# Two transformer layers on one core: VectorE takes the third bank of some score units, with new ranks for the instruction planner

## Chip, cores and metric

The kernel runs on one core of a Trainium2 chip. The metric is device time in microseconds (us): the median of the runs of one program. Engine names in the profile: PE is TensorE's matmuls and PEld its weight loads, DVE is VectorE, ACT is ScalarE, POOL is GpSimd, SP is SyncE (here it issues DMAs).

## What is computed

Two identical layers work on x, a sequence of 2048 rows of 448. Each layer is an attention block (16 heads of 28) and then a mixer block with a gelu MLP (inner size 1792). Inputs and output are bf16.

```python
def _A_ref(x, wqkv, wo):                     # attention
    q, k, v = ...                            # x @ wqkv, 16 heads of 28
    scores = jnp.einsum("bhqd,bhkd->bhqk", q, k) * (Dh ** -0.5)
    p = _softmax(scores, axis=-1)
    o = jnp.einsum("bhqk,bhkd->bhqd", p, v)
    return (heads of o side by side) @ wo
def _B_ref(x, w1, w2, w3, w4):               # mixer and MLP
    h = _gelu(_layernorm(x) @ w1)
    ... # the four quarters of h's columns, shifted by +1, -1, +2, -2 rows
    x1 = x + hs                              # hs = shifted h @ w2
    return x1 + _gelu(_layernorm(x1) @ w3) @ w4
# the whole, twice:
x = x + _A_ref(_layernorm(x), A_wqkv, A_wo)
x = x + _B_ref(_layernorm(x), B_w1, B_w2, B_w3, B_w4)
```

## The kernel before, in words

**Work.** The 2048 rows are 16 tiles of 128. The 16 heads are four groups g of four heads (j = 0 to 3). Queries are taken in chunks of tiles (`CHUNKS`): per layer L three of four tiles, ch 0 to 2, and two of two tiles, ch 3 and 4. `ORDER` cuts each chunk's keys into ranges, so that attention can begin before all keys exist. One range of one chunk for one g is a segment; `segs` lists 32 segments of layer 0 and then 36 of layer 1. A segment's scores come in blocks of 128 keys by 512 columns of one head: 512 queries, or twice 256 with two key tiles in the two-tile chunks. Four blocks, one for each j, make a key block kb. There are 1024 blocks per layer, 2048 in `stream`.

**Score units.** `t_scores` (from L1440) walks the stream. Even units take three blocks in PSUM banks 0, 1, 2, odd units two blocks in banks 3, 4 (`unit_banks`). `score_ops` (L1311) issues their matmuls, the blocks of a unit side by side on different rows of the array. `t_exp` (L1541) exponentiates a whole unit with one ScalarE activation from PSUM into the buffer PT, which holds six units. The scores of unit u wait for the exponential of unit u-2, and the exponential of unit u for PV of unit u-6. `t_pv` (L762 is the line of its matmuls, which come from the helper `mm`) multiplies by V in bank 5. `t_norm` copies the sums out (L1620, L1622) and divides by the softmax's denominator.

**Exponentials on VectorE.** For some blocks VectorE computes the exponential. At each unit, `t_scores` looks 5 or 6 key blocks ahead. If in the planner's account PE spent 15% or more of the last 8 us on filler (`FTH`), the segment has had fewer than `D_RATE[L, ch] * (kb + 1) * 4` such blocks, at most two (`DPK`) of the key block are taken, and a spare bank (b6 or b7), an integer buffer y and an output buffer pd are free, that block is scored with the unit and leaves the stream. Only four-tile chunks take part. `d_first` (L1393) turns the scores into integers in y and releases the bank; `d_chain` (L1431, L1433, L1435, L1438) evaluates a cubic and puts the exponent bits in. Two y buffers exist; more y, f and pd buffers lie in parts of vaug (V with a column of ones) that are unused at the time (`t_extra`): phase 0 up to segment 16, phase 1 after the last PV of layer 0 (event kvfree) up to segment 61. A second branch of `d_chain` on POOL has all its rates at 0.

**The rest of a layer.** After a chunk's attention, `t_outproj` adds the output projection (L1700), `t_mixA` does the first half of the mixer (gelu through tanh with POOL, VectorE and ScalarE, L1787 to L1790), and `t_mixB` the second half for a group of tiles (`BGROUPS`: 0-2, 3-6, 7-10, 11-12, 13-15): `t_mixB1` per tile, then W3 in 14 pieces of 128 features, each with a bank of its own and a VectorE cast (L1933) into h2T, one wide gelu on ScalarE (L1955), and W4 with the residual. In layer 1 a second buffer for it ("h2W") is made of slots of vaug and kT. After the last exponential ("tail") ScalarE takes gelu directly from PSUM (L1929). `t_ln1_l1` normalizes tiles for layer 1 and stores them by DMA.

**What sets the order.** The order of each engine's instructions is written at build time by a planner (`Sched`, a list scheduler with costs in us for every operation). Every piece of work is a generator, spawned with a rank; of candidates that could start at about the same time the lower rank goes first. The ranks of Q, K/V, mixer halves and the rest come from `RANK`, 1.1 to 2.8 in steps of 0.05 over a list of 35 (kind, L, ch); scores have 0, PV 1. The planner also fills PE's idle time with matmuls on the identity (L1996, `keep_pe_busy`). At run time each engine works its list in order, with semaphore waits from the planner's read and write sets.

## Time and profile before

| what | us |
|---|---|
| three runs: median, lowest, highest | 1064.31, 1063.14, 1071.81 |
| span of the profiled execution, first to last instruction | 1061.2 |
| the median less that span | 3.1 |
| ScalarE busy | 1017.8 |
| of it exponentials (L1541, 803 instructions) | 919.4 |
| PE busy, of it filler (L1996) | 990.3, 144.8 |
| VectorE busy, POOL busy | 628.6, 309.1 |
| first exponential starts, last ends | 17.5, 1017.4 |

The profiled execution is one of its own; of it the span is known, and the time around the span is taken as the 3.1 us that separate it from the median. In the profile, "xN" is a count, the figures after a bar are busy us and mean ns of one instruction, and the figures after the second bar are the idle time of the engine just before them and what ended it. Means of one instruction include overlap with the next, so the busy time of a group is less than count times mean.

### The profile page before, as it was taken

Reading aid. Unit: us, or ns where it says so; the run is one execution under the profiler, and the core shown is the slowest. Engines: PE = TensorE matmul, PEld = TensorE weight load, DVE = VectorE, ACT = ScalarE, POOL = GpSimd, SP = SyncE. Lnnn points to the kernel's source line nnn. Section 1 sums busy time; section 2 is a strip of 40 time slices with the busy share of each in tenths; the row PEclk is TensorE's granted clock in tenths of the full one; section 3 lists DMA queues with packets and bytes.
Section 4 is the critical chain, followed back from the end, with each engine's and each line's share of the span. In section 5 each row is a group of like instructions: output and inputs, shape, how many; then the busy total and the mean of one; then the engine's idle time right before and its main releaser. Section 6 shows DMA issues by size and latency. Waiting matters only on the chain.

```text
span 1061.2 us, 34191 instructions
## 1 busy us (share of the span) xinstructions
PE 990.3 (93%) x15418; PEld 405.6 (38%) x15421; DVE 628.6 (59%) x1275; ACT 1017.8 (96%) x921; POOL 309.1 (29%) x510
## 2 busy tenths in 40 slices
PE   6999999989999899999999999999899999999898
PEld 2333433333333444443333333343233334444465
DVE  7777887874574336665455644767686632644433
ACT  6999999999999999999999999999999999999962
POOL 2343112532451022652122301111754300432112
PEclk9999999999999999999999999999999999999999
DMA  4555232230220031220121132423411110221000
GB/s 116 131 131 192 73 65 74 43 66 22 67 60 20 21 96 32 50 38 22 35 86 42 45 91 72 149 69 94 89 25 26 43 38 16 54 54 18 16 15 24
DMA packets 96642, 64.29 MB, mean 61 GB/s; under 512 B 68656, under 2 KB 85376, under 8 KB 96496
## 3 DMA queue, kind: packets, MB, share of 16 engines
q1 hardware_dynamic: 93120, 54.02, 20.2%
q0 software_dynamic: 3376, 8.09, 2.8%
q8 instruction: 121, 1.98, 0.8%
q14 instruction: 25, 0.20, 0.1%
HBM read 28.16 MB, written 16.76 MB: 42 GB/s over the span
## 4 chain that ended last, share of the span: by engine, by line
ACT 75%; PE 16%; DVE 4%; DMA 2%; POOL 1%; issue 1%; SPq 0%; DVEq 0%
ACT PT L1541 68%; PE ps L771 9%; PE ps L1311 4%; ACT h2T L1955 3%; PE ps L762 3%; ACT fb L1789 1%; ACT L1955 1%; ACT L1541 1%; DMA xT<-xnd 1%; DVE st L949 1%; DMA rT<-ub 0%; DMA PT<-in_A_wqkv_dram 0%; DMA xT<-xn 0%; PE ps L1996 0%; ACT vaug L1955 0%
## 5 line engine op out<-in xcount | busy, mean ns | idle before, releaser
L1541 ACT ACTIVATE PT<-ps 128x1536 bf16<-128x1536 f32 (+1 forms) x803 | 919.4, 1342 | 7.1 <-PE ps L1311 6.6
L1311 PE MATMUL ps<-qT,kT 32*128 32x512 bf16 (+1 forms) x2560 | 314.2, 340 | 36.0 <-ACT PT L1541 26.7
L762 PE MATMUL ps<-PT,vaug 128*32 128x512 bf16 (+1 forms) x2518 | 249.2, 340 | 1.0 <-DVE ub L1622 1.0
L1311 PEld LDWEIGHTS ps<-qT,kT 32*128 32x128 bf16 x2560 | 80.5, 91 | 314.4 <-ACT PT L1541 291.8
L771 PE MATMUL ps<-xT,w 128*32 128x512 bf16 (+2 forms) x1952 | 148.3, 357 | 2.9 <-DMA xT<-xn 1.1
L1996 PE MATMUL ps<-ident 128*32 128x256 bf16 x3188 | 144.8, 274 | 2.3 <-POOL ident L851 1.5
L762 PEld LDWEIGHTS ps<-PT,vaug 128*32 128x32 bf16 x2518 | 75.0, 95 | 93.5 <-issue 77.6
L1646 POOL TENSOR_TENSOR otn<-ub,fb 128x512 bf16<-128x512 f32 (+1 forms) x36 | 41.6, 1157 | 236.2 <-DMA fb<-rscr 223.6
L1933 DVE CAST h2T<-ps 128x384 bf16<-128x384 f32 (+2 forms) x98 | 58.3, 595 | 87.7 <-PE ps L771 77.9
L771 PE MATMUL ps<-w,h2T 128*32 128x448 bf16 x1400 | 99.0, 363 | 7.8 <-ACT h2T L1955 7.8
L1996 PEld LDWEIGHTS ps<-ident 128*32 128x32 bf16 x3188 | 89.5, 96 | 28.9 <-issue 12.7
L771 PEld LDWEIGHTS ps<-xT,w 128*32 128x32 bf16 (+1 forms) x1952 | 53.0, 95 | 47.9 <-issue 23.7
L1098 POOL TENSOR_TENSOR sq<-kT 128x512 bf16<-128x512 bf16 (+2 forms) x32 | 30.0, 937 | 116.6 <-DVE kT L1112 114.4
L1787 POOL TENSOR_TENSOR fb<-hT 112x512 f32<-112x512 bf16 (+1 forms) x36 | 37.4, 1042 | 71.7 <-DVE hT L1770 66.3
L771 PEld LDWEIGHTS ps<-w,h2T 128*32 128x32 bf16 x1400 | 37.4, 97 | 42.2 <-issue 15.9
L1098 POOL TENSOR_TENSOR sq<-qT 128x512 bf16<-128x512 bf16 x28 | 29.6, 1060 | 58.7 <-DVE qT L1145 54.2
L1620 DVE COPY ub<-ps 128x512 f32<-128x512 f32 (+1 forms) x40 | 23.3, 583 | 35.0 <-PE ps L762 34.4
L1873 POOL TENSOR_TENSOR x_res<-x_res,x1b 128x448 f32<-128x448 f32 x32 | 38.1, 1193 | 18.6 <-DVE xn L969 18.6
L771 PE MATMUL ps<-xT,wk_pad 128*32 128x512 bf16 (+1 forms) x512 | 42.5, 376 | 0.5 <-DVE kmaxc L1123 0.4
L1700 DVE TENSOR_TENSOR x_res<-x_res,ps 128x448 f32<-128x448 f32 x32 | 19.8, 619 | 38.9 <-PE ps L771 38.6
L771 PE MATMUL ps<-xT,wq_pad 128*32 128x512 bf16 x448 | 41.4, 392 | 0.8 <-DMA xT<-xnd 0.6
L771 PE MATMUL ps<-wo_pad,otn 128*32 128x448 bf16 x512 | 38.9, 361 | 2.5 <-DVE x_res L1700 2.0
(191 smaller groups left out, 1174.0 us busy)
## 6 DMA issues: line engine op xcount, KB each, us to landing
uscr<-ub SPq DMA_DIRECT2D x28, 256.0 KB, 2.0
ub<-uscr SPq DMA_DIRECT2D x28, 256.0 KB
fb<-rscr SPq DMA_DIRECT2D x24, 256.0 KB
xnd<-xn SPq DMA_DIRECT2D x28, 128.0 KB, 2.0
x_res<-in_A_x_dram POOLq DMA_DIRECT2D x16, 224.0 KB, 3.2
xd<-x_res SPq DMA_DIRECT2D x16, 224.0 KB, 2.6
x_res<-xd SPq DMA_DIRECT2D x16, 224.0 KB, 2.8
out_dram<-obf SPq DMA_DIRECT2D x16, 112.0 KB
```

The source lines that it names most:

```text
L762: return lambda e: e.matmul(out=out, lhsT=lhsT, rhs=rhs, start=start, stop=stop, **kw)
L771: r.append(e.matmul(out=out[c:c + w, :], lhsT=lhsT[:, c:c + w], rhs=rhs, start=start, stop=stop, tile_position=(0, c)))
L1098: return op("pool", 0.15 + NW * 0.0018, lambda e: e.tensor_tensor(out=sq[:, si, 0:NW], in0=src, in1=src, op=ALU.mult), reads=rk, writes=[( ...
L1311: yield op("pe", max(0.055, 0.22 / nc_ * NW / 512.0), lambda e, i=i, kc=kc, j=j, g=g, a=a, NW=NW, bank=bank: e.matmul(out=ps[:, bank, i * ...
L1541: yield op("act", 0.06 + n * w * 0.000833, lambda e, bk=bk, s0=s0, n=n, w=w: e.activation(out=PT[:, s0:s0 + n, 0:w], in_=ps[:, bk[0]:bk[0] ...
L1620: yield op("dve", c_ps(NW), lambda e: e.tensor_copy(out=u, in_=ps[:, 5, 0:NW]), reads=[("ps", 5)], writes=[uk])
L1646: yield op("pool", 0.2 + NW * 0.0021, lambda e: e.tensor_tensor(out=otn[:, g, 0:NW], in0=u, in1=rb[:, 0:NW], op=ALU.mult), reads=[uk, fk], ...
L1787: yield op("pool", 0.2 + NW * 0.00165, lambda e: e.tensor_tensor(out=f, in0=z, in1=z, op=ALU.mult), reads=hk, writes=[fk])
L1873: yield op("pool", 1.2, lambda e: e.tensor_tensor(out=X, in0=X, in1=X1, op=ALU.add), reads=[xk, ("x1b", s)], writes=[xk], deps=[nop_])
L1933: ev = op("dve", c_ps(NW), lambda e, hr=hr, vw=vw, b=b: e.tensor_copy(out=hr, in_=vw(ps[:, bi(b), 0:NW])), reads=[("ps", bi(b))], writes=h ...
L1955: yield op("act", c_act(len(fr_) * NW), lambda e, v=v: e.activation(out=v, in_=v, func=ACT.Gelu_apprx_tanh), reads=allk, writes=allk, tab= ...
L1996: return [e.matmul(out=ps[32 * c:32 * c + 32, bi(b), 0:256].rearrange("p (a n) -> p a n", n=128), lhsT=ident[:, 32 * c:32 * c + 32], rhs=i ...
```

## The change

1. **Third bank to VectorE.** In an even unit, before the third block is taken from the stream, the planner's VectorE load over the last 6 us (`DWIN`) is looked up. If it is under 0.7 (`DTH`), a block 5 or 6 key blocks ahead is sought under a second table of rates, `R_RATE`. If y and pd buffers are free, that block's scores go to bank 2, and ScalarE's unit has two blocks. `d_first` doesn't release the bank; it signals dx, and unit u+2 waits for that. For this no filler share and no spare bank are asked for.
2. **Rates of the old way** are new, and the two-tile chunks take part. The POOL branch goes. The chain's rank before it is urgent goes from 1.5 to 2.5.
3. **Own wide buffer.** In layer 0 the W3 result of tiles 11-12 lies in vaug slots 9 to 15 once kvfree has come, instead of in h2T; phase 1 of the extra buffers then opens only when W4 of these tiles is done.
4. **Two-tile W3.** Two 256-column pieces share a bank, and one cast or gelu takes both.
5. **Ranks.** Single values of three decimals in `RANK`. V, LN1 of layer 1, the output projection, `t_mixB1` and W4 (now `t_w4`) get their own ("v", "l", "o", "c", "w"), where they had those of K, K, mixer half A, mixer half B and mixer half B. `Q_LEAD` (how many segments ahead queries are projected) changes too.
6. **Planner.** The costs of 256-column score and PV matmuls change by a few per cent; the bookkeeping of candidates is rewritten without a new rule.

The core of the diff (`RANK` cut to the entries that are spoken of):

```diff
@@ -310,6 +312,14 @@
         self.fills = [x for x in self.fills if x > t]
         return len(self.fills) * 0.12 / win
 
+    def load(self, eng, win):
+        t = self.clock - win
+        busy = 0.0
+        for (e, a, b, _) in reversed(self.log[-150:]):
+            if e == eng and b > t:
+                busy += b - max(a, t)
+        return busy / win
+
     def keep_pe_busy(self, until):
         if self.fill is None:
             return
...
-DPRIO = 1.5
+DPRIO = 2.5
...
-PRATE = {(0, 0): 0, (0, 1): 0, (0, 2): 0, (0, 3): 0, (1, 0): 0, (1, 1): 0, (1, 2): 0}
-XSHUT = (16, 61)
+R_RATE = {(0, 0): 0, (0, 1): 0.01, (0, 2): 0, (0, 3): 0, (0, 4): 0, (1, 0): 0, (1, 1): 0.03, (1, 2): 0.01, (1, 3): 0, (1, 4): 0.04}
+RLO = 5
+RHI = 7
+RPRIO = 1
+DWIN = 6.0
+DTH = 0.7
...
-RANK = {k: round(1.1 + 0.05 * i, 3) for i, k in enumerate([..., ('a', 1, 2), ...])}
+RANK = {..., ('a', 1, 2): 1.166, ..., ('b', 1, 2): 2.769, ('b', 1, 3): 2.461, ..., ('o', 1, 2): 2.439, ('c', 1, 2): 2.409, ('w', 1, 2): 2.844, ('c', 1, 3): 2.317, ('w', 1, 3): 2.98, ...}
-Q_LEAD = {(0, 1): 8, (0, 2): 5, (0, 3): 5, (1, 0): 5, (1, 1): 7, (1, 2): 3, (1, 3): 5}
-D_RATE = {(0, 0): 0.08, (0, 1): 0.045, (0, 2): 0.05, (0, 3): 0, (1, 0): 0.015, (1, 1): 0.1, (1, 2): 0.03}
+Q_LEAD = {(0, 1): 8, (0, 2): 7, (0, 3): 10, (1, 0): 8, (1, 1): 11, (1, 2): 3, (1, 3): 4}
+D_RATE = {(0, 0): 0.1, (0, 1): 0.055, (0, 2): 0.035, (0, 3): 0.03, (0, 4): 0.03, (1, 0): 0.025, (1, 1): 0.095, (1, 2): 0.045, (1, 3): 0.005, (1, 4): 0.045}
...
+SMALL = [11, 12]
...
@@ -1350,7 +1365,7 @@
             return []
 
         def t_extra(ph, base):
-            yield ("wait", ("vinit",) if ph == 0 else ("kvfree",))
+            yield ("wait", ("vinit",) if ph == 0 else ("h2xfree",) if SMALL else ("kvfree",))
             yield ("sig", ("xopen", ph))
             yield ("wait", ("segstart", XSHUT[ph]))
             yield ("sig", ("xshut", ph))
@@ -1388,16 +1403,18 @@
         PDS = ["pd%d" % i for i in range(NPD)]
         YS = ["y0", "y1"]
 
-        def d_first(blk, bank, ys, pd):
+        def d_first(blk, bank, ys, pd, ring=None):
             y, yk = ybuf(ys)
             yield op("dve", c_ps(512), lambda e: e.tensor_scalar(out=y, in0=ps[:, bi(bank), :], scalar1=SCALE * L2E * FS, scalar2=-126.0 * FS, op0=ALU.mult, op1=ALU.max),
                      reads=[("ps", bi(bank))], writes=yk, touch=[bank])
-            yield ("rel", bank)
+            if ring is None:
+                yield ("rel", bank)
+            else:
+                yield ("dead", bank)
+                yield ("sig", ("dx", ring))
             yield ("spawn", d_chain(blk, ys, pd), DPRIO)
 
         at = [0, 0]
-        flying = [0]
-        bypool = set()
 
         def d_chain(blk, ys, pd):
             si, kb, _ = blk
...
@@ -1450,14 +1454,59 @@
             pos = 0
             u = 0
             taken = {}
-            while pos < len(stream):
+
+            def ahead_of(si0, kb0, rates, lo, hi, used):
+                for ahead in range(lo, hi):
+                    si, kb = si0, kb0 + ahead
+                    while si < len(segs) and kb >= len(seg_kb[si]):
+                        kb -= len(seg_kb[si])
+                        si += 1
+                    if si > si0 + DSEG or si >= len(segs):
+                        return None
+                    L, ch, g = segs[si][0:3]
+                    rate = rates.get((L, ch), 0)
+                    if not rate:
+                        return None
+                    js = [j for j in range(4) if (si, kb, j) not in home and j not in used]
+                    if taken.get((si, kb), 0) >= DPK or not js:
+                        continue
+                    if taken.get((si, id(rates), 0), 0) >= rate * (kb + 1) * 4:
+                        continue
+                    if any(("k", L, g, kc_of(L, kt)) not in SC.events for kt in seg_kb[si][kb]):
+                        return None
+                    if si > si0 and (("q", L, CHUNKS[L][ch][0] // 4, g) not in SC.events or (not segs[si][5] and ("qp", si) not in SC.events)):
+                        return None
+                    return (si, kb, js[0])
+                return None
+
+            def take(blk, rates, slot):
+                home[blk] = pbuf(slot)
+                taken[(blk[0], id(rates), 0)] = taken.get((blk[0], id(rates), 0), 0) + 1
+                taken[blk[0:2]] = taken.get(blk[0:2], 0) + 1
+
+            ringed = set()
+            while True:
                 if u == 1:
                     yield ("acq", ["b3"])
                     yield ("acq", ["b4"])
                 if u >= 2:
                     yield ("wait", ("ex", u - 2))
+                if u - 2 in ringed:
+                    yield ("wait", ("dx", u - 2))
                 un = []
-                while pos < len(stream) and len(un) < 3 - u % 2:
+                rb = None
+                lim = 3 - u % 2
+                while pos < len(stream) and len(un) < lim:
+                    if len(un) == 2 and rb is None and SC.load("dve", DWIN) < DTH:
+                        rb = ahead_of(un[-1][0], un[-1][1], R_RATE, RLO, RHI, [b_[2] for b_ in un])
+                        got = None
+                        if rb is not None:
+                            got = yield ("try", [xtra("y") + YS, xtra("pd") + PDS])
+                        if got is not None:
+                            take(rb, R_RATE, got[1])
+                            ringed.add(u)
+                            break
+                        rb = 0
                     blk = stream[pos]
                     pos += 1
                     if blk in home:
...
+                if u in ringed:
+                    blks.append(rb)
+                    banks.append(2)
+                    extra.append((rb, ("b2", got[0], got[1], u)))
+                if SC.idle_share(8.0) >= FTH:
+                    blk = ahead_of(si0, kb0, D_RATE, DLO, DHI, [b_[2] for b_ in blks])
+                    if blk is not None:
                         got = yield ("try", [MISC[0:2], xtra("y") + YS, xtra("pd") + PDS])
+                        if got is not None:
+                            take(blk, D_RATE, got[2])
+                            blks.append(blk)
+                            banks.append(bi(got[0]))
+                            extra.append((blk, got))
                 yield from score_ops(blks, banks)
                 for blk, got in extra:
+                    yield ("spawn", d_first(blk, *got), 1 if len(got) == 3 else RPRIO)
                 yield ("sig", ("st", u))
                 u += 1
             units.append([])
...
@@ -1892,7 +1915,13 @@
                 for xs in slots:
                     yield ("rel", xs)
             wide = False
-            if direct:
+            hname = None
+            small = L == 0 and tiles == SMALL
+            if small:
+                yield ("wait", ("kvfree",))
+                hb = vaug[:, 9:16, :].rearrange("p a b -> p (a b)").rearrange("p (f w) -> p f w", w=NW)
+                hkey = [[("vaug", 9 + k) for k in range(f * NW // 512, (f * NW + NW - 1) // 512 + 1)] for f in range(14)]
+            elif direct:
                 hb, hkey = PT, [[("pt", f)] for f in range(14)]
             else:
                 hname = yield ("acq", ["h2T", "h2W"] if ("xdone", 1) in SC.events else ["h2T"], [("xT", xt)])
...
+            parts = [list(range(f, min(f + fps, 14))) for f in range(0, 14, fps)]
+            if wide:
+                parts = [p for q in parts for p in ([f for f in q if f < 7], [f for f in q if f >= 7]) if p]
+            for fs in parts:
+                m = len(fs)
+                for k, fch in enumerate(fs):
+                    for fc in FCS:
+                        yield op("pe", c_mm(NW), (mm4 if NW > 300 else mm)(ps[:, bi(b), k * NW:(k + 1) * NW], w3[:, fc, 128 * fch:128 * fch + 128], xv(xt)[:, fc, 0:NW], fc == 0, fc == 3),
+                                 reads=[("xT", xt), ("w3",)], writes=[("ps", bi(b))], touch=[b], mode="col4" if NW > 300 else "plain")
+                hk = []
+                for f_ in fs:
+                    hk += [k for k in hkey[f_] if k not in hk]
+                pv = ps[:, bi(b), 0:m * NW].rearrange("p (f w) -> p f w", w=NW)
+                if wide and fs[0] >= 7:
+                    hr = kT[:, 0:n, 128 * (2 + fs[0]):128 * (2 + fs[0] + m)].rearrange("p a (f r) -> p f a r", r=128)
+                    pv = pv.rearrange("p f (a r) -> p f a r", r=128)
+                else:
+                    hr = vaug[:, 9 + fs[0]:9 + fs[0] + m, 0:NW] if wide else hb[:, fs[0]:fs[0] + m, 0:NW]
+                if m == 1:
+                    hr, pv = hr[:, 0], pv[:, 0]
+                    ev = op("dve", c_ps(m * NW), lambda e, hr=hr, pv=pv: e.tensor_scalar(out=hr, in0=pv, scalar1=0.5, scalar2=None, op0=ALU.mult),
+                    ev = op("act", c_act(m * NW), lambda e, hr=hr, pv=pv: e.activation(out=hr, in_=pv, func=ACT.Gelu_apprx_tanh),
+                    late.extend(fs)
+                    ev = op("dve", c_ps(m * NW), lambda e, hr=hr, pv=pv: e.tensor_copy(out=hr, in_=pv),
...
+            yield ("spawn", t_w4(L, tiles, hcol, hkey, late, direct, soft, small, wide, hname), RANK["w", L, ch])
+
+        def t_w4(L, tiles, hcol, hkey, late, direct, soft, small, wide, hname):
-            if not direct:
+            if small:
+                yield ("sig", ("h2xfree",))
+            elif not direct:
...
-                SC.spawn(t_outproj(L, ch), RANK["a", L, ch])
+                SC.spawn(t_outproj(L, ch), RANK["o", L, ch])
```

## The prediction, made before the result was known

> **What bounds the kernel now.** I read the page's first two parts, then the chain of work that ended last, then the costly groups with their shapes kept apart, then busy time by stretches and the tail's timeline.
>
> ```profile
> PE 990.3 (93%) x15418; PEld 405.6 (38%) x15421; DVE 628.6 (59%) x1275; ACT 1017.8 (96%) x921; POOL 309.1 (29%) x510
> ...
> ACT  6999999999999999999999999999999999999962
> ...
> ACT 75%; PE 16%; DVE 4%; DMA 2%; POOL 1%; issue 1%; SPq 0%; DVEq 0%
> ```
>
> ScalarE is full from the second slice to the 38th, and three quarters of the chain is its own work. PE's 93% deceives: the keep-busy matmuls on the identity (L1996) are 144.8 us of it, so 845.5 us is work.
>
> ```profile
> L1541 ACT ACTIVATE PT<-ps 128x1536 bf16<-128x1536 f32 x401 | 623.2, 1554 | 6.7 <-PE ps L1311 6.3
> L1541 ACT ACTIVATE PT<-ps 128x1024 bf16<-128x1024 f32 x401 | 453.6, 1131 | 0.4 <-PE ps L1311 0.3
> ...
> L1541 ACT ACTIVATE PT<-ps 128x512 bf16<-128x512 f32 x1 | 0.7, 703 | 0.0
> ```
>
> These are the softmax exponentials, in units of three and two blocks of 128x512. ScalarE waits for scores only 7 us in all. 3x401 + 2x401 + 1 = 2006 blocks are ScalarE's. The stream has 2048, and the other 42 are VectorE's:
>
> ```profile
> L1393 DVE TENSOR_SCALAR yd<-ps 128x512 int32<-128x512 f32 x26 | 17.9, 687 | 25.7 <-PE ps L1311 25.6
> ...
> L1393 DVE TENSOR_SCALAR vaug<-ps 128x512 int32<-128x512 f32 x16 | 11.0, 687 | 7.0 <-PE ps L1311 6.8
> ```
>
> The stretches show what cover there is, and the tail. Columns: window, length, busy time of PE, its weight loads, DVE, ACT, POOL.
>
> ```profile
> 46.00:75.00 29.00, 28.62 (x375) 9.07 (x367) 21.61 (x48) 28.90 (x27) 13.51 (x17) 1.00 0.41 98
> ...
> 165.00:250.00 85.00, 77.79 (x1205) 31.04 (x1206) 64.15 (x111) 83.29 (x76) 29.92 (x45) 1.00 0.22 44
> ...
> 753.00:881.00 128.00, 122.38 (x1764) 44.34 (x1757) 77.67 (x137) 127.27 (x114) 47.56 (x70) 1.00 0.14 35
> ```
> ```profile
> 1017.00:1062.00 45.00, 40.98 (x756) 25.69 (x754) 16.96 (x36) 15.30 (x34) 9.66 (x21) 1.00 0.06 20
> ```
>
> The last exponential ends at 1017.35 us; the 43.8 us after it are PE's (40.98 busy of 45). So two things can shorten the time: blocks taken off ScalarE before 1017, and a shorter tail.
>
> **The change, part by part.** The profile's span is 1061.2 us; the median of the three runs is 1064.3, 3.1 us around the span. I take every term off both alike.
>
> *Price of a block on ScalarE.* The exponential group is busy 919.4 us for 2006 blocks: 0.458 us a block. A block gone from the stream saves that. A third bank handed to VectorE turns a 1536 instruction into a 1024 one: 1554 - 1131 = 0.423 us.
>
> *Price on VectorE.* Five steps by their rows: L1393 0.69, L1431 0.70, L1433 0.77, L1435 0.53, L1438 0.73 = 3.4 us a block. Beside ScalarE this is hidden while VectorE has room, as 753 to 881 does (77.7 of 128). Without cover it costs 3.4 instead of saving 0.42.
>
> *How many more blocks.* (1) The third-bank rates allow, per segment, the rate times its blocks, rounded up: (0,1) 8, (1,1) 12, (1,2) 4, (1,4) 8, so 32 at most. They need buffers and a planned VectorE load under 0.7 over 6 us, but no idle PE. Where (0,1) runs, VectorE is at 75% in both windows shown (21.61 of 29, 64.15 of 85), so I take half there; elsewhere it is at 61% or less, so all: 4 + 24 = 28. (2) The old way (a spare bank, and at least 15% of filler on PE) allowed 108 and got 42. The new rates, with the two-tile chunks let in, allow 132; at the same success that is 51, +9. Bounds: -10 (less filler once ScalarE is quicker) and +90 (all granted). I take +9, which the 42 of 108 is nearest to. Sum: 28 x 0.423 + 9 x 0.458 = 11.8 + 4.1 = **15.9 us** off ScalarE, with 37 x 3.4 = 126 us more for VectorE (628.6 to about 755, 72%).
>
> [...]
>
> *The new wait.* A third bank is refilled two units later, so those scores now wait for L1393 as well as for the activation. Queued behind them on PE are all PV and projection matmuls, and ScalarE waits for the scores. Slack: scores are written while the unit before is exponentiated, and the bank is wanted when its own shorter activation ends, 2 x 0.458 = 0.9 us after that starts. L1393 takes 0.69 and may start one VectorE instruction (0.7) late. The 42 of today met a ready score 27 times of 42 (L1393 idled 15 times, 32.3 us), in banks that nothing hurried. Bounds for a stall: 0 and 1 us for each third bank. I take 0, since ScalarE's whole wait for scores is 7 us over 803 instructions; the upper end is a rival below.
>
> *Given back near the end.* Chunk (1,4) is the last 128 blocks, 128 x 0.458 = 59 us before 1017. There PE has no filler from 960 to 1000 and 0.9 us from 1000 to 1040, so the PE work displaced goes into the tail. Its 8 third banks (3.4 us) I give back: -15.9 becomes **-12.5**.
>
> *Tail and order.* The three-decimal ranks separate out-projection, LN1, V, the second mixer half and the W4 step from their old common rank. They reorder PE and VectorE, and with them the queued DMAs: the xn transposes, xd and xnd stores on SP, whose queue already waits for VectorE results (97 us at L1634 alone), and small power steps on POOL. DMA holds 2% of the chain and POOL 1%, so these moves cost nothing unless a stalled SP issue holds up a transpose; then 2.9 us each, the row of xT<-xn. What can count: mixing of chunk (1,2) goes from rank 2.4 to 1.166, ahead of most. Its first work comes after 881, when PE has 5.96 + 4.97 = 10.9 us of filler (880 to 960), while W3/W4 for tiles 7 to 12 spill past 1017. Best end -10.9. Worst end +5.8, the three runs of W4 matmuls for tiles 11-12 at 1034 to 1040 (4.72 + 0.75 + 0.37), if their rank of 2.98 makes them last. Between, I take **-3**.
>
> *Two-tile W3.* 14 casts of 256 columns (0.423) per layer become 7 of 512 (0.691): 5.9 to 4.8 us of VectorE in layer 0. In the tail 14 gelus of 0.384 halve in number, but ScalarE waits for PE there (9.3 + 8.3 us). Nothing on the path; if the last pair of gelus is exposed, +0.3.
>
> *Own wide buffer.* Tiles 13-15 of layer 0 need not wait for tiles 11-12. Their gelus ran at 643.2 and 598.4, so up to 45 us are opened, but ScalarE is never idle there (55.94 of 56, 31.95 of 32): 0. The extra VectorE buffers open later in layer 1: two first steps ran from 520 to 640, at most 2 x 0.458 = 0.9 lost. The matmul costs in the planner change no instruction by themselves. The removed POOL branch had all rates 0: nothing.
>
> Sum: -12.5 - 3 = -15.5. 1061.2 becomes 1045.7 in the span, and 1064.3 becomes **1049 us**.
>
> **Rivals.** *PE takes over as bound.* For: no filler 520 to 560 and 840 to 880, almost none 600 to 640. Against: ScalarE still did not wait there. If third banks in (1,1), (1,2) and (1,4) pay half, 24 x 0.423 / 2 = 5.1 is lost instead of 3.4, and without the tail's 3 the gain is 10.8; if PE also takes half of the old-way blocks' 4.1, 8.7: 1056 us.
>
> *The third banks hardly come.* If plan load or the pair of integer buffers lets only one in four of my 28 through, 7 x 0.423 + 4.1 = 7.1 and the tail unchanged: 1057; if the filler blocks also fall by 10 (-4.6 for +4.1), 3.0 - 4.6 = -1.6: 1066. For it: the old way got 42 of 108. Against: no filler and no spare bank is asked for.
>
> *All that is allowed comes.* 32 x 0.423 + 40 x 0.458 = 31.9 us, near 1032. VectorE would need 245 us more; against it, its windows up to 250 us are at 73 to 83%.
>
> *Slower, by the bank-2 wait.* Place: the score matmuls two units after each third bank. VectorE runs in order, and one queue of two instructions in front of L1393 is 1.4 us, 0.5 beyond the slack. If each of 28 waits cost 1 us on ScalarE's path: -15.5 + 28 = +12.5, 1077. It decides for slower than before from 15.5 / 28 = 0.55 us a third bank, and for slower by 1% from 0.93.
>
> **How the numbers follow.** Forecast 0.52, its own range 1041 to 1056. PE as bound 0.16; few third banks 0.10; all of them 0.08; the wait 0.14. Left out of 1034 to 1070 are half of the 1032 case and a little more below (0.06), and the upper part of the wait (0.11): 0.17. A measurement of this kernel tells about 1% from no change (10.6 us, so 1053.7 and 1075). Faster: 0.43 of the forecast, 0.05 of PE as bound, 0.03 of few, 0.08 of all: 0.59. Slower: 0.10 of the wait. The same: 0.31.
>
> **What would show it.** L1541 with 1024 columns more numerous than with 1536 by twice the third banks or so; about 79 first steps instead of 42; DVE near 755 us; the last exponential at about 1004; ScalarE's wait for L1311 still under 10 us; L1311 seldom released by the first step. The tail from the last exponential to the end near 44 us. Wrong: waits of L1311 on VectorE that sum above 10 us, a tail over 50, or fewer than 55 first steps.

## The result and the profile after

The median fell from 1064.31 to 1059.16 us (9 runs each, 1061.44 to 1071.81 and 1056.30 to 1064.23): a ratio of 0.994, 95% interval 0.9915 to 0.9966. That is 0.6% faster, by the bound of 1% the same; the forecast was 1049. The profiled execution has a span of 1057.7 us against 1061.2, so 3.5 us are to be accounted for where 15.5 were forecast. Lines of the code move: scores L1311 are L1326 now, the exponential L1541 is L1564, the first step L1393 is L1408, the chain is L1435, L1437, L1439 and L1442, the matmul helpers are L777 and L786, the filler is L2035.

The page of the changed kernel, busy time and the chain that ended last:

```profile
PE 983.3 (93%) x15301; PEld 400.4 (38%) x15301; DVE 735.8 (70%) x1432; ACT 1001.9 (95%) x907; POOL 327.9 (31%) x510
...
ACT  7999999999999999999999999999899999999952
...
ACT 55%; PE 26%; DVE 12%; DMA 3%; POOL 3%; issue 1%; SPq 0%; DVEq 0%; POOLq 0%
```

ScalarE looks as full as before, but it makes up only 55% of the chain instead of 75%; VectorE has gone from 4% to 12%, PE from 16% to 26%. The groups of the exponentials and of VectorE's first steps, shapes kept apart:

```profile
L1564 ACT ACTIVATE PT<-ps 128x1536 bf16<-128x1536 f32 x380 | 587.7, 1547 | 11.1 <-PE ps L1326 9.7
L1564 ACT ACTIVATE PT<-ps 128x1024 bf16<-128x1024 f32 x416 | 460.7, 1122 | 3.8 <-PE ps L1326 3.7
```
```profile
L1408 DVE TENSOR_SCALAR yd<-ps 128x512 int32<-128x512 f32 x53 | 35.8, 681 | 24.7 <-PE ps L1326 24.6
...
L1408 DVE TENSOR_SCALAR vaug<-ps 128x512 int32<-128x512 f32 x22 | 15.1, 685 | 10.2 <-PE ps L1326 10.0
```

53 + 22 = 75 blocks are VectorE's, 33 more than the 42 of before. In the order of the 797 units 18 that should carry three banks carry two: these are the third banks, the other 57 came the old way. The page sums the exponential to 905.8 us where it was 919.4, so 13.6 us are off ScalarE. The last exponential ends at 1005.09 instead of 1017.35, 12.3 earlier, and the tail behind it is 52.6 us instead of 43.8. ScalarE waits for scores twice as long. Before and after (us in total, times, longest):

```profile
ACT PT L1541 <- PE ps L1311: 6.6, 9, 1.8
```
```profile
ACT PT L1564 <- PE ps L1326: 13.4, 22, 2.5
```

The stretches show where (columns as in the prediction, then PE's granted clock, the DMA engines' share and GB/s):

```profile
46.00:75.00 29.00, 28.00 (x351) 8.79 (x349) 23.17 (x49) 28.96 (x27) 14.73 (x17) 1.00 0.38 105
...
165.00:250.00 85.00, 75.97 (x1102) 28.39 (x1097) 70.71 (x117) 78.80 (x72) 34.91 (x49) 0.96 0.20 44
753.00:881.00 128.00, 115.90 (x1684) 42.12 (x1676) 97.79 (x167) 123.51 (x111) 53.00 (x82) 1.00 0.25 42
1005.00:1055.00 50.00, 49.42 (x934) 30.60 (x926) 18.18 (x39) 20.16 (x30) 9.73 (x21) 1.00 0.07 21
```

From 165 to 250 us ScalarE was busy 83.29 of 85 before and is 78.80 now, while VectorE went from 64.15 to 70.71. In the tail PE is busy 49.42 of 50. The chain in order of time (start, us, what; "x" the instructions of a piece) shows that it is PE almost alone:

```profile
1010.79 4.91 PE ps L777 x44
...
1019.09 8.44 PE ps L786 x176
...
1029.18 25.61 PE ps L786 x568
...
1054.88 0.68 DVE obf L2020
```

How VectorE holds up ScalarE is seen in a stretch of the timeline (start, us, engine, line; in brackets the idle time before it and what ended it):

```profile
204.18 2.04 POOL L1810 TENSOR_TENSOR fb<-hT 112x512 f32<-112x512 bf16 x2
...
205.25 2.11 DVE L1811 SCALAR_TENSOR_TENSOR fb<-fb,hT 112x512 f32<-112x512 f32 x2 [2.35 <-POOL fb L1810]
...
206.79 0.63 ACT L1812 ACTIVATE fb<-fb 112x512 f32<-112x512 f32 x1 [1.60 <-DVE fb L1811]
207.29 1.27 DVE L1793 TENSOR_SCALAR hT<-ps 112x512 bf16<-112x512 f32 x2
...
208.02 1.90 PE L786 MATMUL ps<-xT,wq_pad 128*32 128x512 bf16 x16 [1.89 <-DVE hT L1793]
```

GpSimd squares for the tanh GELU (L1810), two pieces in a row, and VectorE waits for the first. Its step on that piece (L1811) then runs while GpSimd works on the second square and takes 1.51 us; the next one, alone, takes 0.68. ScalarE's tanh waits 1.60 us for it, VectorE's evacuations (L1793) come behind it, and PE's next projection waits 1.89 us for them. From 207.9 us PE's granted clock is 0.50 for 3.4 us; this is taken up in the last section.

A second stall, 1.34 us before the exponential at 234.8 us, has a DMA in it. PE's projection stood behind the transpose of xn, which was issued at 230.20, when VectorE had just written xn, and landed at 233.57 by the semaphore records; the scores stood behind the projection.

### The profile page after: what moved, and what is told of

Same layout as the page of the kernel before. It is cut to its first block, busy times and chain, and to the rows that moved or that the text cites. A ratio compares the mean times of both kernels' runs of the same rounds, so it can differ in the third digit from the quotient of the medians.

```text
span 1057.7 us, 34104 instructions
## 1 busy us (share of the span) xinstructions
PE 983.3 (93%) x15301; PEld 400.4 (38%) x15301; DVE 735.8 (70%) x1432; ACT 1001.9 (95%) x907; POOL 327.9 (31%) x510
## 3 DMA queue, kind: packets, MB, share of 16 engines
q8 instruction: 120, 1.97, 0.7%
## 4 chain that ended last, share of the span: by engine, by line
ACT 55%; PE 26%; DVE 12%; DMA 3%; POOL 3%; issue 1%; SPq 0%; DVEq 0%; POOLq 0%
ACT PT L1564 49%; PE ps L786 14%; PE ps L1326 6%; PE ps L777 5%; ACT h2T L1989 3%; DMA rT<-ub 1%; DVE PD L1442 1%; DVE fb L1435 1%; ACT fb L1812 1%; DMA fb<-rscr 1%; DVE fb L1437 1%; DVE PD L1439 1%; DVE yd L1408 1%; ACT L1989 1%; DVE vaug L1408 1%
## 5 line engine op out<-in xcount | busy, mean ns | idle before, releaser
L1564 ACT ACTIVATE PT<-ps 128x1024 bf16<-128x1024 f32 (+1 forms) x797 | 905.8, 1324 | 14.8 <-PE ps L1326 13.4
L1326 PE MATMUL ps<-qT,kT 32*128 32x512 bf16 (+1 forms) x2560 | 311.9, 341 | 30.6 <-ACT PT L1564 25.0
L777 PE MATMUL ps<-PT,vaug 128*32 128x512 bf16 (+1 forms) x2471 | 250.0, 341 | 1.0 <-DVE ub L1645 0.9
L1326 PEld LDWEIGHTS ps<-qT,kT 32*128 32x128 bf16 x2560 | 80.0, 91 | 306.0 <-ACT PT L1564 261.8
L786 PE MATMUL ps<-xT,w 128*32 128x512 bf16 (+1 forms) x2048 | 154.2, 360 | 2.3 <-DVE PD L1439 1.8
L2035 PE MATMUL ps<-ident 128*32 128x256 bf16 x3068 | 136.6, 275 | 7.8 <-DVE yd L1408 2.5
L777 PEld LDWEIGHTS ps<-PT,vaug 128*32 128x32 bf16 x2471 | 73.9, 95 | 95.4 <-issue 78.3
L2035 PEld LDWEIGHTS ps<-ident 128*32 128x32 bf16 x3068 | 84.3, 96 | 36.6 <-issue 13.8
L786 PE MATMUL ps<-w,h2T 128*32 128x448 bf16 x1288 | 87.2, 361 | 7.8 <-ACT h2T L1989 7.4
L1971 DVE CAST h2T<-ps 128x384 bf16<-128x384 f32 (+1 forms) x84 | 52.3, 623 | 60.3 <-PE ps L786 59.8
L1669 POOL TENSOR_TENSOR otn<-ub,fb 128x512 bf16<-128x512 f32 (+1 forms) x36 | 43.3, 1202 | 145.1 <-DMA fb<-rscr 139.1
L786 PEld LDWEIGHTS ps<-xT,w 128*32 128x32 bf16 x2048 | 55.0, 95 | 49.5 <-issue 25.9
L1810 POOL TENSOR_TENSOR fb<-hT 112x512 f32<-112x512 bf16 (+1 forms) x36 | 37.9, 1056 | 73.3 <-DVE hT L1793 68.7
L1113 POOL TENSOR_TENSOR sq<-kT 128x512 bf16<-128x512 bf16 (+2 forms) x32 | 31.4, 988 | 86.2 <-DVE kT L1127 84.1
L1113 POOL TENSOR_TENSOR sq<-qT 128x512 bf16<-128x512 bf16 x28 | 32.4, 1159 | 77.3 <-DVE qT L1160 69.9
L1408 DVE TENSOR_SCALAR yd<-ps 128x512 int32<-128x512 f32 x53 | 35.8, 681 | 24.7 <-PE ps L1326 24.6
L786 PEld LDWEIGHTS ps<-w,h2T 128*32 128x32 bf16 x1288 | 35.1, 97 | 37.7 <-issue 15.1
L786 PE MATMUL ps<-xT,wq_pad 128*32 128x512 bf16 x512 | 44.4, 395 | 2.4 <-DVE hT L1793 1.9
L786 PE MATMUL ps<-xT,wk_pad 128*32 128x512 bf16 (+1 forms) x512 | 44.2, 377 | 0.0
L1896 POOL TENSOR_TENSOR x_res<-x_res,x1b 128x448 f32<-128x448 f32 x32 | 39.2, 1229 | 14.5 <-DVE xn L984 14.3
L970 POOL TENSOR_SCALAR vpe<-mv 128x1 f32<-128x1 f32 (+2 forms) x21 | 6.7, 318 | 114.5 <-DVE mv L965 114.5
L1885 POOL TENSOR_SCALAR mst<-mv 128x1 f32<-128x1 f32 x32 | 9.1, 288 | 102.2 <-DVE mv L965 101.9
```

Source lines behind the costliest of these rows:

```text
L777: return lambda e: e.matmul(out=out, lhsT=lhsT, rhs=rhs, start=start, stop=stop, **kw)
L786: r.append(e.matmul(out=out[c:c + w, :], lhsT=lhsT[:, c:c + w], rhs=rhs, start=start, stop=stop, tile_position=(0, c)))
L1113: return op("pool", 0.15 + NW * 0.0018, lambda e: e.tensor_tensor(out=sq[:, si, 0:NW], in0=src, in1=src, op=ALU.mult), reads=rk, writes=[( ...
L1326: yield op("pe", (0.005 + NW * 0.00042) / nc_, lambda e, i=i, kc=kc, j=j, g=g, a=a, NW=NW, bank=bank: e.matmul(out=ps[:, bank, i * NW:(i + ...
L1408: yield op("dve", c_ps(512), lambda e: e.tensor_scalar(out=y, in0=ps[:, bi(bank), :], scalar1=SCALE * L2E * FS, scalar2=-126.0 * FS, op0=A ...
L1564: yield op("act", 0.06 + n * w * 0.000833, lambda e, bk=bk, s0=s0, n=n, w=w: e.activation(out=PT[:, s0:s0 + n, 0:w], in_=ps[:, bk[0]:bk[0] ...
```

## The experiments

My theory was that VectorE, with more to do, is late, and that PE and then ScalarE wait for it; and that at the end PE is the bound, so that what ScalarE gains there is lost. Rivals: a narrow wait in the new code (the filler that waits for first steps), the third banks themselves, and the new order by itself. All ratios are to the kernel before, run beside it on the same chip.

**VectorE made light.** Three of the four chain steps work on 32 columns, and the one between them, still 512 wide, reads the integers instead of the polynomial; no instruction is out of its place. VectorE's exponentials are then not computed. The same cut was made in the kernel before.

```diff
-scalar_tensor_tensor(out=q, in0=lo, scalar=E2 / E3 * FS, in1=lo, ...)
+scalar_tensor_tensor(out=q[:, 0:32], in0=lo[:, 0:32], scalar=E2 / E3 * FS, in1=lo[:, 0:32], ...)
```

> The changed kernel, order of every engine as planned, but VectorE's chain cut short: of its four steps after the first, three work on 32 columns instead of 512 (the polynomial and the exponent are left out for the other columns), so VectorE has about 75 x 1.9 = 140 us less to do. The wait theory (the extra VectorE work makes VectorE late, PE's queue waits for its evacuations, and ScalarE for the scores) expects ScalarE's wait for scores to fall from 13.4 us to 7 or less and the time to fall by 6 to 12 us, to 1047 to 1053. The end theory (PE is the bound from the last chunks on, so what ScalarE saves comes back as a longer tail) expects less than 3 us, and a tail still near 52 us.

> The kernel before with the same cut (three of the four chain steps on 32 columns, the rest of those columns left out): 42 x 1.9 = 80 us less for VectorE. It tells how much of a gain in the run before comes from any lighter VectorE. The wait theory expects less here than in the changed kernel: 1 to 4 us. The end theory expects under 2 us in both.

The changed kernel so cut: 1049.74 us (1048.83 to 1051.19), ratio 0.9855 [0.983, 0.988], span 1048.3. The kernel before so cut: 1065.07, ratio 0.9989 [0.9959, 1.0018]. In the changed kernel the span falls by 9.4 us, in the one before there is no gain clear of noise (1 to 4 us had been expected). The wait for scores, 8.0 us where I had named 7 or less, and the same stretch as above, in the light run:

```profile
ACT PT L1564 <- PE ps L1326: 8.0, 9, 2.7
```
```profile
165.00:250.00 85.00, 78.72 (x1180) 30.41 (x1180) 57.27 (x121) 83.63 (x77) 30.32 (x48) 1.00 0.20 44
```

ScalarE is back at 83.63 of 85. The first wide GELU starts at 256.7 us here and at 263.2 in the changed kernel; the fifth at 619.3 against 627.4, the end at 1048.3 against 1057.7: 6.5 us, then 8.1, then 9.4. Two thirds arise before 263 us.

**The filler that waits for first steps.** In the changed kernel filler (L2035) waits 13.0 us, 19 times, for L1408; before, 1.3. Here the 27 groups of filler that stand behind a first step are left out (they compute nothing that is used).

> The changed kernel, order as planned, without the 27 groups of filler matmuls that write a bank right after VectorE's first step has read it (108 matmuls on the identity, no result uses them). In the trace of the changed kernel such fillers wait 13.0 us for the first step, 19 times, against 1.3 us before. The wait theory, in its narrow form (the filler holds up the scores behind it), expects ScalarE's wait for scores to fall by 3 to 6 us and the time by 2 to 6. In its broad form (projections and PV wait for VectorE as well) it expects under 2. The end theory expects under 1.

1058.78 us, ratio 0.9944 [0.9922, 0.9965]: the same as the changed kernel. ScalarE still waits 12.5 us. Filler that waits costs nothing that can be measured; the rival falls.

**The end.** The exponentials of the last chunk (1,4) on 64 of 512 columns, so that most of it is not computed and ScalarE has 40 us less to do (busy 961.8 instead of 1001.9).

> The changed kernel, order as planned, but the exponentials of the last chunk (1,4), 128 blocks less those of VectorE, do only 64 of 512 columns (the others are left out), so ScalarE has some 40 us less in the last 58 us before its last exponential. The end theory expects PE to be as full as before: at most 4 us off the time, with the last exponential earlier and the tail longer by nearly the same. If ScalarE is the bound there, 20 us or more come off.

1056.64 us, ratio 0.992 [0.9896, 0.9945], span 1056.3. ScalarE's 40 us are worth 1.4 us of span, and 2 to 3 us between executions of both at a clock of 0.995; it waits for PE instead:

```profile
ACT PT L1565 <- PE ps L1326: 47.8, 63, 2.9
```

In the last stretch PE is the bound, as the theory has it.

**Amount or order.** Four planned anew: (a) no third banks and the old rates, with the new ranks, buffer and sharing; (b) third banks and new rates with the old ranks and leads, without the own buffer and the sharing; (c) the changed kernel without third banks alone; (d) planned with the chain's measured durations.

```diff
(a), (c)  -R_RATE = {..., (1, 1): 0.03, (1, 2): 0.01, (1, 3): 0, (1, 4): 0.04}
          +R_RATE = {}
(a) too   D_RATE as before
(b)       RANK, Q_LEAD, DPRIO as before; SMALL = []; fps = 1
(d)       -DST = [('dve', 0.6), ('dve', 0.6), ('dve', 0.34), ('dve', 0.6)]
          +DST = [('dve', 0.72), ('dve', 0.77), ('dve', 0.47), ('dve', 0.74)]
```

> The changed kernel with no third banks and the old rates, so about 45 blocks on VectorE; ranks, own buffer and shared banks stay as changed. Amount theory (the additional blocks make VectorE late): ScalarE waits for scores as little as before (about 7 us), the last exponential comes 30 x 0.44 = 13 us later than in the changed kernel, less the 9 us that a lighter VectorE was worth, so the time is 1060 to 1066. Order theory (the new order makes VectorE late with the old number too): the waits stay at 12 us or more and the time is 1066 to 1073.

> The kernel before with third banks and new rates alone: the changed kernel's code with the old ranks, leads and chain rank, no own buffer, no shared banks, about 75 blocks on VectorE. Amount theory: ScalarE's wait for scores rises to 12 us or more, the last exponential comes no more than 8 us earlier than before (1017.4). Order theory: the waits stay near 7 us and the last exponential comes 13 us or more earlier, at 1004 or before. By both the tail is longer than 44 us where PE was already full at the end, so the time is 1054 to 1066.

> The changed kernel without third banks, its own rates kept: about 62 blocks on VectorE. If third banks are worth what their blocks are (13 x 0.43 = 5.6 us of ScalarE), it is 1062 to 1068 with the last exponential at 1008 to 1012. If they pay for themselves with waits, it is 1055 to 1061 and ScalarE's wait for scores is under 10 us.

> The changed kernel, planned with the durations of VectorE's chain steps that the profile shows (0.72, 0.77, 0.47, 0.74 us for 0.60, 0.60, 0.34, 0.60). The planner then puts 67 blocks on VectorE instead of 75, in another order. If VectorE is late because the planner takes it for quicker than it is, ScalarE's wait for scores falls to 8 us or less. The ranks were chosen for the other costs, so the tail may be longer than 52.6 us, and the time 1054 to 1066.

| order | blocks on VectorE | us | ratio | ScalarE's wait for scores | mean granted clock, profiled execution |
|---|---|---|---|---|---|
| before | 42 | 1064 to 1067 | 1 | 6.6 | 0.997 |
| new (a) | 45 | 1069.86 | 1.0049 [1.0029, 1.0069] | 9.8 | 0.998 |
| old (b) | 75 | 1095.79 | 1.0281 [1.0245, 1.0317] | 39.1 | 0.969 |
| new (c) | 62, none a third bank | 1070.30 | 1.0051 [1.0033, 1.0069] | 19.5 | 0.992 |
| new (d) | 67 | 1071.28 | 1.0044 [1.0021, 1.0067] | 15.3 | 0.978 |
| changed | 75 | 1059.16 | 0.994 [0.9915, 0.9966] | 13.4 | 0.995 |

(a) has the first wide GELU at 258.9 us, so with few blocks the new order is not late there. But its 1069.86 misses the 1060 to 1066 that I had named for the amount of blocks as cause and lies in the 1066 to 1073 named for the order. Its clock was high, so it shows that the new ranks without the new blocks lose. (b), (c) and (d) lie above every range that I had named for them. (c) has waits of 19.5 us without a third bank, so third banks are not needed for them.

The 30 us that the new blocks lose in the old order (b) can't be laid to the order alone. In its profiled execution the clock was 0.50 for 68 us, 27 of them in one piece:

```profile
1004.40:1031.70 27.30, 27.30 (x234) 10.07 (x236) 13.45 (x29) 20.66 (x21) 2.45 (x4) 0.50 0.01 1
```

An estimate from the mean clock: (1 - 0.969) x 1096.9 = 34 us of PE's time, as much as (b) lost, and 23 us in (d), against 5 in the changed kernel. Every re-planning also changes when hundreds of instructions meet. How much of the 11 to 37 us over the changed kernel is order and how much clock was not separated, and none of these runs alone can be read as the worth of the part taken out.

**Why VectorE is late.** Take VectorE's instructions that run more than 0.2 us over the lower quartile of their kind. In the changed kernel they overrun by 35.7 us in sum (50 instructions; before 17.6, 28 of them), and all of them ran beside an instruction of GpSimd. This is not a matter of the blocks alone: the four plans above have 30 to 33 us, (a) with its 45 blocks 31.1. And the light run, with 20.4, lost collisions as well as load, so it doesn't part the two. So GpSimd's work was cut, in the order as planned: first its two squares (norms of K and Q, tanh GELU) and the residual addition on 32 columns, in both kernels (VectorE's step behind the GELU's square then reads its other input twice).

```diff
-tensor_tensor(out=sq[:, si, 0:NW], in0=src, in1=src, op=ALU.mult)
+tensor_tensor(out=sq[:, si, 0:32], in0=src[:, 0:32], in1=src[:, 0:32], op=ALU.mult)
```

> The changed kernel with three of GpSimd's operations (the squares for the norms of K and Q, the square in the tanh GELU, one residual addition) cut to 32 columns, so that part of the norm, of the GELU and of the residual is not computed; all instructions stay in their order. My theory that VectorE is late mainly because its instructions are stretched while GpSimd runs: VectorE's instructions run over their usual length by well under 35 us in sum, and 4 to 9 us of the 9.4 us come back: 1050 to 1055 us. The rival, that VectorE simply has too much work in the first 260 us: under 2 us back, 1057 to 1060 us.

> The kernel before with the same cut of GpSimd's three operations (part of the norm, of the GELU and of the residual is not computed). By both theories VectorE is not what it waits for, so under 2 us either way: 1062 to 1066 us.

1051.85 us, ratio 0.9862 [0.9831, 0.9892]; the overrun falls to 11.7 us. In the kernel before 1064.87, ratio 0.9989 [0.9963, 1.0015]: nothing. But the squares also stand on a path (VectorE, GpSimd, PE), which got shorter. So they were then replaced by memsets, which read nothing and were meant to last as long; the residual addition stayed on 32 columns:

```diff
-tensor_tensor(out=sq[:, si, 0:NW], in0=src, in1=src, op=ALU.mult)
+[memset(sq[:, si, i:min(i + 86, NW)], 1.0) for i in range(0, NW, 86)]
```

> As the run with GpSimd's operations cut (the residual addition on 32 columns), but the two squares, for the norms of K and Q and for the tanh GELU, are replaced by six memsets each over the same output, so that GpSimd stays busy about as long and passes its result on about as late, and only reads nothing there (so the norms and the GELU are not computed). If VectorE was late because both engines read SBUF together: VectorE's instructions run over their usual length by far less than 35 us, and 1050 to 1054 us. The rival, that only the shorter path through GpSimd's squares brought the 7 us: 1056 to 1060 us.

1050.23 us, ratio 0.985 [0.98, 0.99], span 1047.7, overrun 12.2 us. GpSimd's groups in that run:

```profile
L1113 POOL MEMSET sq<- 128x86 bf16 (+1 forms) x340 | 41.7, 170 | 177.0 <-DVE kT L1127 91.0 <-DVE qT L1160 80.2 <-PE ps L786 3.7
L1810 POOL MEMSET fb<- 112x86 f32 x180 | 22.5, 173 | 86.2 <-DVE hT L1793 80.8 <-DVE hT L1813 5.2
```

The means include overlap: by the timeline six memsets in a row take 0.72 us, where the square of 512 columns took 1.04. So the path through GpSimd was 0.32 us shorter, not as long as it was. The run before had shortened it further, its square of 32 columns taking 0.24 us, and gained no more. And beside memsets alone VectorE's steps keep their usual length: L1437 0.68 us in 6 cases, L1442 0.68 in 10. So by this run the squares' reads are most of it (overrun 12.2 us where it was 35.7), but the shorter path has a share. The first stretch of the timeline above, in this run, shows both:

```profile
203.14 1.38 POOL L1810 MEMSET fb<- 112x86 f32 x12
...
203.89 1.36 DVE L1811 SCALAR_TENSOR_TENSOR fb<-fb,hT 112x512 f32<-112x512 f32 x2 [2.01 <-POOL fb L1810]
...
204.62 0.63 ACT L1812 ACTIVATE fb<-fb 112x512 f32<-112x512 f32 x1 [0.41 <-DVE fb L1811]
...
205.91 1.05 PE L786 MATMUL ps<-xT,wq_pad 128*32 128x512 bf16 x16 [0.79 <-DVE hT L1793]
```

ScalarE's tanh waits 0.41 us instead of 1.60. Of the difference 0.83 us is L1811 no longer stretched, and 0.32 is L1811 beginning 0.75 us after GpSimd instead of 1.07. From 165 to 250 us VectorE does nearly as much as in the changed kernel, and ScalarE is full:

```profile
165.00:250.00 85.00, 78.26 (x1176) 30.18 (x1174) 68.24 (x120) 83.41 (x78) 27.43 (x89) 1.00 0.20 44
```

Where the collisions cost was asked by the same edit for GpSimd's instructions of the first 260 us alone:

> As the run whose GpSimd squares only write, but only for GpSimd's instructions that are planned in the first 260 us (some 21 squares for the norms, 5 of the GELU and a few residual additions, which are therefore not computed); all later ones are those of the changed kernel. If the loss arises in the first 260 us and is carried along, as the first wide GELU starting 6.5 us later in the changed kernel than in the run with light VectorE work suggests: 5 to 7 us come back, 1052 to 1054 us, and that GELU starts near 257 us. The rival, that it arises by small amounts everywhere: 1 to 3 us, 1056 to 1058 us.

1055.10 us (1051.64 to 1058.38), ratio 0.9908 [0.9873, 0.9943]. In the profiled execution the first wide GELU starts at 257.1 us, the fifth at 620.4 (7.0 early) and the span is 1050.6: there the early part carries 7 us to the end. The four runs spread over 7 us, and their interval overlaps the changed kernel's. They part by the granted clock: two executions at 0.998 have spans of 1049.9 and 1050.6, those at 0.995 and 0.990 have 1056.1 and 1056.6. That the early part counts most is what the profile says; how much of it reaches the median stays open.

**Other ranks for more blocks.** Two complete kernels, with only RANK, Q_LEAD, R_RATE and D_RATE other than in the changed one:

```diff
-R_RATE = {(0, 1): 0.01, (1, 1): 0.03, (1, 2): 0.01, (1, 4): 0.04, ...}
+R_RATE = {(0, 1): 0.04, (0, 2): 0.03, (0, 4): 0.03, (1, 0): 0.02, (1, 1): 0.02, (1, 2): 0.03, (1, 3): 0.05, (1, 4): 0.03, ...}
```

> The complete kernel, with other ranks, leads and rates (nothing else differs from the changed kernel), chosen so that the plan stays short when VectorE's instructions run late at random. About 90 blocks on VectorE by plan instead of 75 (15 x 0.45 = 6.7 us more off ScalarE). If the loss was the fit between plan and VectorE's lateness, it falls with the re-planning and the time goes to 1045 to 1052 us. The rival, seen in the four re-planned runs before, that any other set of blocks or ranks costs 5 us or more on the chip because the collisions with GpSimd fall anew: 1062 to 1080 us.

> A second complete kernel of the same kind with another set of ranks, leads and rates: about 96 blocks on VectorE by plan (21 x 0.45 = 9.5 us more off ScalarE than in the changed kernel). By the first theory 1045 to 1053 us, by the rival 1062 to 1080 us. If VectorE's total load decides, this one, with more of it, is slower than the one with 90.

The first, with 90 blocks, took 1066.24 us, ratio 1.001 [0.9994, 1.0026]; the second (its rates are those in the diff), with 96, took 1058.13, ratio 0.994 [0.9913, 0.9967], the changed kernel's to the third decimal. ScalarE has 7 and 10 us less exponential to do by number of blocks (15 and 21 x 0.45), and waits for scores 25.9 and 24.7 us instead of 13.4; VectorE's overrun is 39.4 and 39.6 us. The first is in the range of my rival (1062 to 1080), the second between both. Their clock was lower too: the medians of the ten executions are 0.982 and 0.989, against 0.995 in the changed kernel. Near one clock they are not behind: at 0.992 two executions of the second have spans of 1053.3 and 1053.7 us, one of the changed kernel 1059.6; at 0.988 one of the first has 1060.1, and one of the changed kernel at 0.990 has 1062.5. So what is gained on ScalarE is given back together with longer waits and a lower clock; which of these brings the other was not tried. No version that was run is clearly faster than the changed kernel.

## Why the prediction was wrong

*Price of a block and how many: right in sum, the split was not.* 28 third banks and 9 old-way blocks were forecast, 18 and 15 came: 18 x 0.423 + 15 x 0.458 = 14.5 us by my prices, 13.6 measured, 15.9 forecast. That the sum is near is luck: too many of one kind and too few of the other cancel.

*"Beside ScalarE this is hidden while VectorE has room": the step that failed.* I judged the room by VectorE's share of a stretch (75%) and took a stall of 0, looking for one only at the third bank's refill. "61% or less" elsewhere was misread, too: from 713 to 753 us VectorE was busy 30.63 of 40 before the change, 77%. The wait at the refill did not come: no score matmul is released by L1408 in the whole profile. But VectorE, 83% busy from 165 to 250 us (70.71 of 85), passed its delays on to what was queued behind them: evacuations for PE, and by PE's own order the scores. At 207.29 us the evacuations (L1793) started behind L1811, 1.81 us after the last projection matmul ahead of them had ended (205.48). Measured: 9.4 us of span by the run with light steps, where I had put 0. Part of it goes with the granted clock, for which I had no term: at 0.998 one execution of the changed kernel has a span of 1054.6 us, two of the light run 1047.1 and 1048.3, one with memsets 1049.2, which leaves 5.4 to 7.5 us. I also priced VectorE's steps by their means in the kernel before and did not ask what else ran beside them: L1437 took 1.14 us on the mean beside GpSimd's large operations and 0.68 otherwise.

*"Tail and order, -3": failed too.* The tail is 52.6 us, +8.8, above the 50 that I had named as a sign of error. Before, the last two wide GELUs, for tiles 7 to 10 of layer 1 (6.4 us, and 2.6 for two table loads), started at 997.9 and 1001.0, ahead of the last exponential, and now start at 1006.9 and 1010.0, behind it. So 9 of the 12.3 us by which the last exponential ends earlier are only this move, and -12.5 was met for another reason than mine. PE has hardly a pause after 1005, and 40 us less of ScalarE work in the last chunk bring 1.4 to 3: there PE is the bound.

*The sum.* Off ScalarE 13.6; lost with VectorE's lateness, the clock included, 9.4; the rest, 13.6 - 9.4 - 3.5 = 0.7 us lost, is what tail and order come to. With the lateness removed by either cure the kernel takes 1049.7 or 1050.2 us, which is near the forecast; but both cures leave work out.

*The rivals.* "PE takes over as bound" (1056) was nearest in time, and PE's share of the chain rose, and behind the last exponential PE is the bound; but its reason, third banks that pay half because PE has no filler, isn't what the runs show. "Hardly come" and "all come" were out by number, 33 more blocks. "Slower, by the bank-2 wait" named the right engine and the wrong place.

*The edits costed at nothing.* The own buffer, the two-tile sharing and the moved DMAs were not tried one by one; in (a) they came with the new ranks and lost 5 us together, in a plan that differs throughout. That the moved DMAs cost nothing doesn't hold everywhere: the stall at 234.8 us stands behind a transpose, issued as soon as VectorE had written xn and landed 3.37 us later. What each does alone stays open.

## What to carry to other kernels

Work moved to an engine with spare time was not hidden here where others waited for that engine's queue (VectorE at 70% of the span, but 83% from 165 to 250 us; 9.4 us of span): look in the busiest stretch at who waits for its evacuations, not at its mean share. When an order is fitted to a plan, undoing a part re-plans all of it; keep the instructions in place and shrink them to find what a load costs. Look at what runs on GpSimd beside VectorE before pricing VectorE by the mean of a quiet kernel (its instructions overran by 17.6 us in the kernel before, by 35.7 in the changed one). And compare executions of like granted clock: 0.992 and 0.998 were 5 us apart in one and the same kernel here.

## What the runs showed of the hardware

**VectorE and GpSimd.** A row of L1437 (two SBUF inputs), in the changed kernel and in the run whose squares only write (ns: least, median, longest):

```profile
L1437 DVE SCALAR_TENSOR_TENSOR fb<-fb,vaug x14: 670/684/1530, 117.2 to 809.6; 128x512 f32<-128x512 f32 x14
```
```profile
L1437 DVE SCALAR_TENSOR_TENSOR fb<-fb,vaug x14: 671/684/693, 117.8 to 800.4; 128x512 f32<-128x512 f32 x14
```

The longest falls from 1.53 to 0.69 us. In the row fb<-fb,yd it stays at 1.77 in both runs; GpSimd's L1669, beside which it ran in the changed kernel, is unchanged in the second. Counted over the changed kernel, L1437 takes 1.14 us on the mean in the 15 cases that overlap one of GpSimd's four large operations (L1113, L1810, L1896, L1669) and 0.68 in the other 60; L1439, with a single SBUF input, 0.80 and 0.42; L984, the same, 1.06 and 0.50; L1408, which reads PSUM, 0.68 either way. GpSimd suffers too: its square of 128x512 takes 1.04 us at the longest in the 29 cases without a chain step, norm or GELU step of VectorE beside it, and up to 1.62 in the other 19.

So L1437 is stretched beside GpSimd's large operations; beside memsets alone it took 0.68 us in 6 cases. L1439 is stretched beside the first too; beside memsets alone it took 0.42 us in 5 cases. The longest delay of a chain step was 1.1 us (L1435 at 714.1 us, 1.77 where 0.68 is usual, beside L1669). Why the two engines stretch each other there was not shown. The cut of GpSimd's reads brought 7 to 9 us of 1058 in the changed kernel, part of it with the clock, and nothing measurable in the kernel before.

**The granted clock.** In the changed kernel's profiled execution the clock is 1.00 from 13.4 us to the end of the work but for three stretches of 3.4 us at 0.50, from 207.9, 235.2 and 382.0 us. The first two with the stretch ahead of each (the last three columns are clock, DMA share, GB/s):

```profile
204.50:207.90 3.40, 1.63 (x17) 0.41 (x14) 2.65 (x4) 1.80 (x3) 1.72 (x2) 1.00 0.00 0
207.90:211.30 3.40, 3.28 (x35) 1.03 (x35) 3.40 (x6) 3.09 (x4) 2.44 (x2) 0.50 0.01 2
231.80:235.20 3.40, 1.60 (x27) 0.58 (x24) 3.30 (x7) 2.06 (x3) 0.66 (x1) 1.00 0.30 17
235.20:238.60 3.40, 3.40 (x34) 0.89 (x28) 1.39 (x3) 2.49 (x3) 0.75 (x1) 0.50 0.02 3
```

Each of the three begins within 1.6 us of the end of a pause of PE: 1.89 us (to 208.02), 1.80 (to 233.76) and 2.29 (to 381.8); the first two are the stalls shown above. An estimate from the clock: 3.4 us at 0.50 cost PE 1.7 us of full speed, 5 us for the three. The 16 projection matmuls that take 1.90 us at 208.02 take 1.05 in the run with memsets, whose mean clock is 1.000. But not every pause has such a stretch behind it: the changed kernel's pauses of 1.97 us (to 268.0) and 2.37 us (to 765.8) are followed by no such stretch, nor are three of 1.97 to 2.29 us in the run with memsets. Over executions of one kernel the time goes with the clock: the changed kernel's nine have spans from 1054.6 us at 0.998 to 1062.5 at 0.990. That the pauses bring the half clock is what the order in time suggests in these three; it was not tried, and so it was not shown that a late VectorE costs twice, by PE's pause and by the half clock behind it.
